# Moving the first batch's feed-forward casts to ScalarE and widening VectorE's third addition of attention weights to the second batch

## The chip, the cores and the metric

The kernel runs on one core of a Trainium2 chip. The metric is the device time of one execution in microseconds (us), the median of several runs. Five engines of the core appear in the profile: TensorE (PE for matmuls, PEld for its weight loads), VectorE (DVE), ScalarE (ACT), GpSimd (POOL) and SyncE (SP, which here only issues transfers). Each works through its own instructions in order, and they wait for one another by semaphores.

## The reference

Two layers follow each other. The first is attention in which a query sees only the keys of its own hash bucket; the second is a feed-forward layer whose hidden values are the largest of three projections.

```python
# q, k, v: (4 batches, 8 heads, 768 positions, 64); proj: (64, 6)
q_bits = (q @ proj > 0);  k_bits = (k @ proj > 0)          # 6 bits give a bucket
mask   = q_bucket[:, :, :, None] == k_bucket[:, :, None, :]
scores = where(mask, q @ k.T / 8, -1e9)
attn   = exp(scores - max);  attn /= attn.sum + 1e-9
x      = (attn @ v) as (3072 tokens, 512)
h      = maximum(maximum(x @ w1, x @ w2), x @ w3)           # w1, w2, w3: (512, 768)
out    = h @ w_out                                          # (768, 512), float32
```

## The kernel before

**Chunks and units.** The queries of a batch are cut into chunks. The first batch (b = 0) has three chunks of 256 queries, c = 0, 1, 2; the other batches have two chunks of 384 each, c = 3 to 8. For each chunk and head, the weights of all 768 keys are made in parts of 768 columns, called units: two units per head in the first batch and three in the others, 48 units per batch and 192 in all. `scores(u)` (line 282) issues three matmuls (256 wide) or two (384 wide) of line 298 into a PSUM tile `sc`, of which there are two, and one exponential on ScalarE (line 306) that writes an fp16 tile `AT`. So the scores of a unit must wait until the exponential of two units before has been read out.

**Sums and values.** When the four heads of a half chunk are done, `burst(c, i)` (line 341) makes their sums of weights with matmuls against a tile of ones (line 358) and the weighted values (line 380). In the first batch the sum takes every one of the six key blocks of a head: 24 matmuls, 32 output rows for each of the four heads. From chunk 3 on, VectorE adds the three units of a head first: `add` (line 322) is called two units after unit 1 and unit 2 of a head and adds whole tiles of 768 columns (line 329). That leaves two blocks of 384 columns per head, so two passes of four matmuls. For chunks from `THIRD_ADD` on, which is 5 here, `add` also adds the two halves to each other (line 332) behind the second addition, and `sum_blocks` (line 334) hands over one block per head: one pass of four matmuls. After the sums VectorE makes reciprocals (lines 365 to 369) and scales the values into `xT` (line 387).

**Feed-forward.** `ffn_groups(c)` (line 402) makes a list of items. An item of the first layer is four matmuls of line 413 for one of six blocks of hidden rows (fb) and one of the three weights (wi) into one of four rotating PSUM banks `ms`. The first weight's result (wi = 0) is cast to fp16 into a tile `ht`; the second and third are taken into it by VectorE's maximum (line 422). The cast is done by ScalarE if the chunk is 384 wide (line 418) and by VectorE if it is 256 wide (line 420). For chunk 0 the items are ordered weight by weight, so that its six casts come from six consecutive items; for the others the three weights of one block follow each other. Items of the second layer are three matmuls of 512 columns (line 457), two items to a row block, with a copy by ScalarE (line 461).

**Order.** The order is written out by hand in the loop over units at the end (line 613). In each turn u it issues `scores(u + 1)`, then whatever is due at u (loads, transposes of later batches by VectorE on line 202, additions), then as many feed-forward items as a credit allows (1 a turn in the first batch, 1.15 afterwards), and last the sums and values that are due. A feed-forward list is appended two turns after the chunk's last values. So the feed-forward of chunk 0 runs in the last units of the first batch, and that of chunks 1 and 2 in the units of the second batch, whose chunks are 3 and 4.

Of the kernel before, what the change touches and what calls it, by code (L numbers as in the profile page):

```python
# [17 lines left out]
def kernel(  # L18
# [12 lines left out]
    nc = tc.nc  # L31
# [4 lines left out]
    HALF = S // 2  # L36
# [15 lines left out]
    EPS = 2.0 ** -60  # L52
    NAT = 24
    SPREAD = {2: (61, 9), 3: (100, 12)}
    THIRD_ADD = 5
    LAG = (1, 4)
    ATW = 776

# [31 lines left out]
    def bank():  # L90
        i = free_banks.pop(0)
        return i, bank_tiles[i]

    def give(i):
        if i is not None:
            free_banks.append(i)
# [182 lines left out]
    def block_of(b, m):  # L279
        return 2 * (m % MH) + m // MH if b == 0 else m  # L280
# [29 lines left out]
    def weights_of(c, h, m):  # L310
        w = chunks[c][2]
        nb = 2 * HALF // w
        return blocks(at_tiles[at_of[unit_at[c, h, m // nb]]], w)[:, m % nb, :]

    def xt_of(c):
        if c not in xts:
            xts[c] = x_pool.tile([P, NJC, HALF], FP16, tag="xT", name="xT")
        return xts[c]
# [3 lines left out]
    def add(c, h, n):  # L322
# [6 lines left out]
        nc.vector.tensor_tensor(out=sum_of[c, h][:], in0=t[0], in1=t[n], op=AluOp.add)  # L329
        if n == 2 and c >= THIRD_ADD:  # L330
            t = sum_of[c, h]
            nc.vector.tensor_tensor(out=t[:, 0, :], in0=t[:, 0, :], in1=t[:, 1, :], op=AluOp.add)  # L332

    def sum_blocks(c, h):
        w = chunks[c][2]
        if (c, h) in sum_of:
            t = sum_of[c, h]
            return [t[:, j, 0:w] for j in range(1 if c >= THIRD_ADD else 2)]
        return [weights_of(c, h, m)[:, 0:w] for m in range(NM)]
# [62 lines left out]
    def ffn_groups(c):  # L402
        b, q0, w = chunks[c]
        xt = xt_of(c)
        hts, gs, l2 = {}, [], {}
        jobs = [(fb, wi) for fb in range(NFB) for wi in range(3)]
        if c == 0:
            jobs = [(fb, wi) for wi in range(3) for fb in range(NFB)]
        for fb, wi in jobs:
            def go(fb=fb, wi=wi):  # L410
                k_, ps = bank()
                for jc in range(NJC):
                    nc.tensor.matmul(ps[:, 0:w], w_sb[wi][:, jc, fb * P : (fb + 1) * P], xt[:, jc, 0:w],  # L413
                                     start=(jc == 0), stop=(jc == NJC - 1))
                if wi == 0:
                    hts[fb] = h_pool.tile([P, HALF], FP16, tag="ht", name="ht")
                    if w == HALF:
                        nc.scalar.copy(hts[fb][:, 0:w], ps[:, 0:w])  # L418
                    else:
                        nc.vector.tensor_copy(hts[fb][:, 0:w], ps[:, 0:w])  # L420
                else:
                    nc.vector.tensor_tensor(out=hts[fb][:, 0:w], in0=hts[fb][:, 0:w], in1=ps[:, 0:w], op=AluOp.max)  # L422
                give(k_)
            gs.append(go)
        rows = out[b * S : (b + 1) * S, :].rearrange("(p c) m -> c p m", c=NM)

        def out_rows(tb):
            if c < NCH - 1:
                return o_pool.tile([P, DM], FP32, tag="osb", name="osb")
            if "end" not in nat:  # L430
                nat["end"] = nat_pool.tile([P, 4 * NM * D], FP32, tag="nat", name="nat")
            return nat["end"][:, tb * DM : (tb + 1) * DM]

        def last(tb, cs, use_act):
            k_, ps = bank()
            n = cs.stop - cs.start
            for fb in range(NFB):
                nc.tensor.matmul(ps[:, 0:n], hts[fb][:, tb * P : (tb + 1) * P], wout_sb[:, fb, cs],  # L438
                                 start=(fb == 0), stop=(fb == NFB - 1))
            osb = out_rows(tb)  # L440
            if use_act:
                nc.scalar.copy(osb[:, cs], ps[:, 0:n])
            else:
                nc.vector.tensor_copy(osb[:, cs], ps[:, 0:n])
            give(k_)
            (nc.scalar if use_act else nc.sync).dma_start(rows[block_of(b, q0 // P + tb)][:, cs], osb[:, cs])

        def item(tb, part):
            def go2(part, tb=tb):
                if c == NCH - 1 and tb == w // P - 1:  # L450
                    last(tb, slice(part * DM // 2, (part + 1) * DM // 2), part == 0)
                    return
                if part == 0:
                    l2[tb] = bank()
                k_, ps = l2[tb]
                for fb in range(part * MH, (part + 1) * MH):
                    nc.tensor.matmul(ps[:, 0:DM], hts[fb][:, tb * P : (tb + 1) * P], wout_sb[:, fb, :],  # L457
                                     start=(fb == 0), stop=(fb == NFB - 1))
                if part == 1:
                    osb = out_rows(tb)  # L460
                    nc.scalar.copy(osb[:, 0:DM], ps[:, 0:DM])  # L461
                    give(k_)
                    nc.sync.dma_start(rows[block_of(b, q0 // P + tb)], osb[:, 0:DM])
            gs.append(lambda: go2(part))

        ntb = w // P
        steps = [(0, 0)]
        for tb in range(1, ntb):
            steps += [(tb, 0), (tb - 1, 1)]
        steps.append((ntb - 1, 1))  # L470
        if c == NCH - 1:
            steps = steps[:-3] + [steps[-2], steps[-3], steps[-1]]
        for tb, part in steps:
            item(tb, part)
        return gs
# [194 lines left out]
```

## Time and profile before

| What | Value |
|---|---|
| Runs before | 264.42, 264.56, 264.79 us; median 264.56 |
| Profiled execution | 264.41 us |
| Span of its instructions | 262.4 us (2.0 us lie around it) |
| Granted TensorE clock | 1.00 |
| Busy | PE 256.5, DVE 207.8, ACT 177.9, POOL 69.8 us |

The profile shows one execution. "Busy" is the time in which at least one instruction of an engine is under way. A timeline row gives start, length, engine, line, operation, output<-input and count; in square brackets stands the idle time of the engine before it and who ended it. Instructions of one engine overlap at their ends, so the distance from one start to the next, called pace below, is shorter than the length that a row gives. A matmul's length is modelled; the starts are what shows how fast TensorE goes.

### The profile page before, as it was taken

To read this page: it belongs to the slowest core of one execution; us is meant where nothing else is said; L and a number is where in the kernel's file an instruction comes from. 1 tells how busy PE (TensorE), PEld (TensorE's weight loads), DVE (VectorE), ACT (ScalarE), POOL (GpSimd) and SP (SyncE) were. 2 spreads that over 40 slices of the span, in tenths; PEclk is the share of its full clock that TensorE was granted. 3 is DMA by queue.
4 is the path that set the end of the run, shared out by engine and by line. 5 is a ranking of instruction groups with operands and counts; after the bars stand their busy time and mean duration, and the time that the engine had idled before them with its cause. 6 is when DMAs were issued, how large, how long until landed. Compare 5 with 4: busy or idle time off the path is not lost.

```text
span 262.4 us, 6477 instructions
## 1 busy us (share of the span) xinstructions
PE 256.5 (98%) x2503; PEld 154.4 (59%) x2503; DVE 207.8 (79%) x492; ACT 177.9 (68%) x258; POOL 69.8 (27%) x132
## 2 busy tenths in 40 slices
PE   8999999999999999999999999999999999999995
PEld 4655658865765666555555554655555555555552
DVE  2897767966799999969999996899849795888350
ACT  3797886667968675956869588584886859581322
POOL 3878752355043526330141612011000000000000
PEclk9999999999999999999999999999999999999999
DMA  6998999979732964970073653802030003000303
GB/s 210 326 224 170 170 235 226 217 132 204 187 91 75 202 139 61 273 186 17 0 198 104 116 127 49 210 0 58 20 122 1 0 2 121 2 0 2 120 0 120
DMA packets 20717, 30.95 MB, mean 118 GB/s; under 512 B 2608, under 2 KB 15248, under 8 KB 20688
## 3 DMA queue, kind: packets, MB, share of 16 engines
q0 software_dynamic: 8128, 13.37, 27.3%
q1 hardware_dynamic: 12128, 16.66, 22.0%
q10 hardware_dynamic: 432, 0.52, 0.6%
q8 instruction: 19, 0.31, 0.5%
q14 instruction: 10, 0.08, 0.1%
HBM read 25.17 MB, written 6.29 MB: 120 GB/s over the span
## 4 chain that ended last, share of the span: by engine, by line
PE 89%; DVE 5%; ACT 3%; issue 2%; DVEq 0%; ACTq 0%
PE ms L413 34%; PE sc L298 22%; PE ms L457 11%; PE ms L380 10%; PE ms L221 3%; ACT AT L306 3%; PE ms L358 3%; PE ms L171 1%; PE ms L123 1%; PE ms L504 1%; DVE ht L422 1%; DVE ad L329 1%; DVE xT L387 1%; PE ms L150 1%; PE ms L438 1%
## 5 line engine op out<-in xcount | busy, mean ns | idle before, releaser
L306 ACT ACTIVATE AT<-sc 128x768 f16<-128x768 f32 x192 | 152.4, 816 | 57.2 <-PE sc L298 53.9
L413 PE MATMUL ms<-xT,w_sb 128*128 128x384 f16 (+1 forms) x648 | 115.0, 307 | 0.3 <-DVE xT L387 0.2
L298 PE MATMUL sc<-S 72*128 72x384 bf16 (+1 forms) x432 | 93.8, 308 | 1.2 <-ACT AT L306 0.9
L413 PEld LDWEIGHTS <-w_sb 128*128 128x128 f16 x648 | 62.7, 97 | 35.9 <-issue 0.4
L422 DVE TENSOR_TENSOR ht<-ht,ms 128x384 f16<-128x384 f16 (+1 forms) x108 | 54.2, 503 | 20.7 <-PE ms L413 10.5
L298 PEld LDWEIGHTS <-S 72*128 72x128 bf16 (+1 forms) x432 | 39.4, 98 | 31.8 <-issue 11.8
L207 POOL TENSOR_SCALAR T<-T 128x768 bf16<-128x768 f32 x24 | 22.8, 951 | 90.2 <-issue 48.4
L457 PE MATMUL ms<-wout_sb,ht 128*128 128x512 f16 x138 | 35.5, 378 | 0.0
L380 PE MATMUL ms<-AT,vo 128*32 128x385 f16 (+3 forms) x840 | 34.2, 308 | 0.0
L380 PEld LDWEIGHTS <-vo 128*32 128x32 f16 x864 | 22.9, 96 | 9.2 <-issue 1.7
L329 DVE TENSOR_TENSOR ad<-ad,AT 128x768 f16<-128x768 f16 x48 | 26.6, 553 | 2.1 <-ACT AT L306 1.3
L202 DVE STREAM_TRANSPOSE T<-nat 128x384 f32<-128x384 f32 x48 | 26.8, 564 | 0.0
L329 DVE TENSOR_TENSOR ad<-AT,AT 128x768 f16<-128x768 f16 x48 | 26.2, 546 | 0.2 <-ACT AT L306 0.2
L418 ACT CAST ht<-ms 128x384 f16<-128x384 f32 x36 | 17.3, 480 | 8.1 <-PE ms L413 8.1
L457 PEld LDWEIGHTS <-ht 128*128 128x128 f16 x138 | 13.3, 97 | 13.0 <-issue 0.3
L387 DVE SCALAR_TENSOR_TENSOR xT<-ms,sv,rb 128x384 f16<-128x384 f32 (+1 forms) x35 | 19.2, 565 | 1.3
L461 ACT COPY osb<-ms 128x512 f32<-128x512 f32 x21 | 12.2, 586 | 7.5 <-PE ms L457 5.8
L332 DVE TENSOR_TENSOR ad<-ad 128x384 f16<-128x384 f16 x32 | 15.5, 484 | 1.1
L137 POOL TENSOR_SCALAR S<-T 64x384 bf16<-64x384 f32 (+1 forms) x23 | 14.1, 616 | 4.9 <-DVE T L132 3.3
L196 POOL DMA_DIRECT2D nat<-in_q_dram x20 | 11.1, 560 | 0.1
L365 DVE STREAM_TRANSPOSE ys<-ms 128x384 f32<-128x384 f32 (+1 forms) x17 | 9.0, 531 | 2.3 <-PE ms L358 2.0
L176 DVE TENSOR_SCALAR S<-ms 6x384 bf16<-6x384 f32 x16 | 8.9, 554 | 2.0 <-PE ms L171 1.2
(52 smaller groups left out, 122.6 us busy)
## 6 DMA issues: line engine op xcount, KB each, us to landing
out_dram<-osb SPq DMA_DIRECT2D x21, 256.0 KB
S<-T SPq DMA_DIRECT2D x48, 96.0 KB
nat<-in_q_dram POOLq DMA_DIRECT2D x20, 192.0 KB, 6.3
vo<-in_v_dram POOLq DMA_DIRECT2D x8, 384.0 KB, 5.8
nat<-in_k_dram POOLq DMA_DIRECT2D x16, 192.0 KB, 5.7
w_sb<-in_moe_w_dram POOLq DMA_DIRECT2D x3, 768.0 KB, 12.8
nat<-in_k_dram SPq DMA_DIRECT2D x10, 192.0 KB
nat<-in_k_dram SPq DMA_DIRECT2D x3, 384.0 KB
```

The lines of the kernel that those rows point to most:

```text
L202: nc.vector.transpose(t32[name][:, u, half * HALF : (half + 1) * HALF], i_)
L207: nc.gpsimd.tensor_scalar(out=t16[name][:, u, :], in0=t32[name][:, u, :], scalar1=RS, scalar2=1.0, op0=AluOp.mult, op1=AluOp.mult)
L298: nc.tensor.matmul(views[j], s_of[kn][0 : D + bits, kx, m * P : (m + 1) * P], s_of[qn][0 : D + bits, qx, q0 : q0 + w], start=True, stop=True)
L306: nc.scalar.activation(t[:, :, 0:w], whole, ActFn.Exp, bias=-SCALE * 0.25 * bits, scale=SCALE)
L329: nc.vector.tensor_tensor(out=sum_of[c, h][:], in0=t[0], in1=t[n], op=AluOp.add)
L332: nc.vector.tensor_tensor(out=t[:, 0, :], in0=t[:, 0, :], in1=t[:, 1, :], op=AluOp.add)
L380: nc.tensor.matmul(av[Q * x : Q * (x + 1), 0:n], v_at[2 * b + i][:, x, cb * D + side : (cb + 1) * D : 2], weights_of(c, 4 * i + x, m)[:, 0 ...
L387: nc.vector.scalar_tensor_tensor(out=xt_of(c)[:, 2 * i + side, 0:w], in0=av[:, 0:w], scalar=sv_of[b, i, side][:], in1=rb[0][:, 0:w], op0=A ...
L413: nc.tensor.matmul(ps[:, 0:w], w_sb[wi][:, jc, fb * P : (fb + 1) * P], xt[:, jc, 0:w], start=(jc == 0), stop=(jc == NJC - 1))
L418: nc.scalar.copy(hts[fb][:, 0:w], ps[:, 0:w])
L422: nc.vector.tensor_tensor(out=hts[fb][:, 0:w], in0=hts[fb][:, 0:w], in1=ps[:, 0:w], op=AluOp.max)
L457: nc.tensor.matmul(ps[:, 0:DM], hts[fb][:, tb * P : (tb + 1) * P], wout_sb[:, fb, :], start=(fb == 0), stop=(fb == NFB - 1))
```

## The change

Two edits are made. All casts of a first weight's result go to ScalarE, also those of the three 256-wide chunks. And `THIRD_ADD` goes from 5 to 3, so that chunks 3 and 4 also get the addition of line 332 and hand over one block per head.

```diff
-    THIRD_ADD = 5
+    THIRD_ADD = 3
...
                 if wi == 0:
                     hts[fb] = h_pool.tile([P, HALF], FP16, tag="ht", name="ht")
-                    if w == HALF:
-                        nc.scalar.copy(hts[fb][:, 0:w], ps[:, 0:w])
-                    else:
-                        nc.vector.tensor_copy(hts[fb][:, 0:w], ps[:, 0:w])
+                    nc.scalar.copy(hts[fb][:, 0:w], ps[:, 0:w])
                 else:
```

The code that reads `THIRD_ADD` is unchanged:

```python
        if n == 2 and c >= THIRD_ADD:                       # in add, line 330
            t = sum_of[c, h]
            nc.vector.tensor_tensor(out=t[:, 0, :], in0=t[:, 0, :], in1=t[:, 1, :], op=AluOp.add)
...
            return [t[:, j, 0:w] for j in range(1 if c >= THIRD_ADD else 2)]   # in sum_blocks, line 338
```

In the instruction lists of the two programs, ScalarE has 18 casts of 128x256 more and VectorE 18 fewer; VectorE has 16 additions of 128x384 more (eight heads of chunk 3 and eight of chunk 4); TensorE has 16 sum matmuls with their 16 weight loads fewer. Nothing else changes its place on any engine, and GpSimd's and SyncE's lists are the same.

## The prediction

> **What bounds the kernel now.** I read the shares of the engines first, then the windows around the change.
>
> ```profile
> span 262.4 us, 6477 instructions
> PE 256.5 (98%) x2503; PEld 154.4 (59%) x2503; DVE 207.8 (79%) x492; ACT 177.9 (68%) x258; POOL 69.8 (27%) x132
> ```
>
> TensorE is the bound: starts in the timeline are 0.11 us apart for 256 columns, 0.16 for 384 and 0.22 for 512, and after 42 us I find only one place (below) where that rhythm breaks by 0.3 us. Work taken from TensorE is saved whole; work moved elsewhere is free until TensorE has to wait. The second row of interest is where the other engines have room, in three windows: the casts of chunk 0, of chunk 1, of chunk 2.
>
> ```profile
> 42.00:47.00 5.00, 4.82 (x45) 4.10 (x44) 3.92 (x12) 5.00 (x7) 1.62 (x5) 1.00 1.17 233
> 66.00:81.00 15.00, 14.86 (x155) 10.65 (x154) 13.59 (x35) 11.75 (x17) 3.51 (x5) 1.00 0.44 116
> 86.00:106.00 20.00, 20.00 (x233) 13.05 (x232) 19.30 (x49) 12.81 (x17) 8.49 (x13) 1.00 0.70 143
> ```
>
> The columns are length, PE, PEld, DVE, ACT, POOL, clock. In the first, ScalarE is busy 5.00 of 5.00 us: just the engine that gets six casts there. In the other two VectorE is close to full (13.59 of 15, 19.30 of 20), and it gets the additions.
>
> **Sums on TensorE: a gain.** In each of the four half chunks of batch 1, two passes of four matmuls become one. The eight matmuls of 72.80 are followed by the values at 73.14, so a pass is 0.17 us, weight loads included. 4 x 0.17 = **-0.67**.
>
> **Chunk 0's casts on ScalarE: a loss.** The timeline there:
>
> ```profile
> 41.91 6.09 ACT L306 ACTIVATE AT<-sc 128x768 f16<-128x768 f32 x8 [3.03 <-PE sc L298]
> ```
> ```profile
> 45.46 0.60 PE L413 MATMUL ms<-xT,w_sb 128*128 128x256 f16 x4
> 45.90 0.49 PE L298 MATMUL sc<-S 70*128 70x256 bf16 x3
> 46.23 0.60 PE L413 MATMUL ms<-xT,w_sb 128*128 128x256 f16 x4
> 46.67 0.49 PE L298 MATMUL sc<-S 70*128 70x256 bf16 x3
> ```
>
> One unit takes TensorE 0.77 us (45.90 to 46.67: 0.33 scores, 0.44 item), and ScalarE starts one exponential per 0.77. Its own limit is 0.71, the distance from an exponential to the next instruction:
>
> ```profile
> 107.75 0.58 ACT L461 COPY osb<-ms 128x512 f32<-128x512 f32 x1
> 108.22 0.83 ACT L306 ACTIVATE AT<-sc 128x768 f16<-128x768 f32 x1
> ...
> 112.31 0.47 ACT L418 CAST ht<-ms 128x384 f16<-128x384 f32 x1
> 112.67 0.83 ACT L306 ACTIVATE AT<-sc 128x768 f16<-128x768 f32 x1
> ```
>
> A 512-wide copy holds ScalarE 0.47 us, a 384-wide cast 0.36; 0.11 less again for 256 wide gives 0.26. The row of a 256-wide copy fits: 0.37 long, against 0.47 to 0.48 for 384 here.
>
> ```profile
> L418 ACT CAST ht<-ms 128x384 f16<-128x384 f32 x36 | 17.3, 480 | 8.1 <-PE ms L413 8.1
> L442 ACT COPY nat<-ms 128x256 f32<-128x256 f32 x1 | 0.4, 372 | 0.1
> ```
>
> With a cast per unit ScalarE needs 0.71 + 0.26 = 0.97 where TensorE gives it 0.77. Step by step: second exponential 42.62 (0.71 after 41.91), first cast 43.33, and from there 0.97 per pair, so the sixth exponential starts at 42.62 + 4 x 0.97 = 46.48. It is 0.81 long, ends at 47.29, and frees the tile for the eighth scores. From the end of an exponential to the scores it frees I find 0.10 to 0.15 where ScalarE sets the pace (17.9 to 18.04, 18.60 to 18.69). The eighth scores so start at 47.41, not 46.67: **+0.75**. The sums and values that follow need no ScalarE and give nothing back; TensorE just does all later work later. Bounds: 0.20 per cast gives +0.5; 0.37, no overlap at all, gives +1.2.
>
> The Trainium skill, "ScalarE: Activation LUTs", section "What ACT_TABLE_LOAD costs", has 186 ns plus 0.833 per element for an instruction with immediate scale and bias, and 93 ns of overlap. By that a 256-wide cast would hold the engine 0.31 us, an estimate, and this term would be +0.95. For 384 it gives 0.51; the trace has 0.48 and a pace of 0.36, so I keep the trace.
>
> **Chunk 1 and 2's casts on ScalarE.** Here one unit in three has a cast. 3 x 0.71 + 0.26 = 2.39 against 3 x 0.77 = 2.30 on TensorE: the first cast after a burst costs about 0.1 (0.26 less the 0.1 of play before scores wait and 0.06 regained per unit), each further one under 0.1, and every turn with two items (credit 1.15) gives 0.44 back. I count +0.3 up to 81 us, +0.1 from 86 to 106, both only if nothing else makes TensorE wait at the same place.
>
> **VectorE in batch 1.** What a third addition costs is shown from chunk 5 on:
>
> ```profile
> 120.45 0.52 DVE L329 TENSOR_TENSOR ad<-ad,AT 128x768 f16<-128x768 f16 x1
> 121.00 0.36 DVE L332 TENSOR_TENSOR ad<-ad 128x384 f16<-128x384 f16 x1
> 121.27 0.55 DVE L422 TENSOR_TENSOR ht<-ht,ms 128x384 f16<-128x384 f16 x1
> ```
>
> It must wait for the addition before it: 0.82 from addition to next instruction, against 0.44 without it (79.99 to 80.42 below). So +0.38 each. A cast frees 0.33 (79.17 to 79.50), or 0.52 where the maximum that reads it stands right behind. Two places decide. The first is the one broken rhythm:
>
> ```profile
> 79.99 0.52 DVE L329 TENSOR_TENSOR ad<-ad,AT 128x768 f16<-128x768 f16 x1
> ...
> 80.26 0.49 PE L298 MATMUL sc<-S 72*128 72x384 bf16 x2
> 80.42 0.94 DVE L422 TENSOR_TENSOR ht<-ht,ms 128x256 f16<-128x256 f16 x2
> ...
> 80.89 0.49 PE L413 MATMUL ms<-xT,w_sb 128*128 128x256 f16 x3
> ```
>
> The item of 80.89 should start at 80.59; it waits for its bank, which the first maximum of 80.42 reads until 80.83. Since its last pause (before 69.41) VectorE would lose three casts (0.52 + 0.33 + 0.33 = 1.18) and gain the third additions of heads 3, 4 and 5 (1.14). The maximum stays where it is, so TensorE's 0.3 of ScalarE waits up to here falls into the 0.30 that it waits now: **0.0** net for chunk 1.
>
> The second is the sum of chunk 4's first half:
>
> ```profile
> 99.39 0.52 DVE L329 TENSOR_TENSOR ad<-ad,AT 128x768 f16<-128x768 f16 x1
> ...
> 100.20 0.51 PE L358 MATMUL ms<-ad,ones 128*32 128x384 f16 x8
> ```
>
> The addition of 99.39 is head 3's second and is done 0.29 before its reader. By then VectorE has lost eight casts since 69.41 (0.52 + 7 x 0.33 = 2.83) and gained eight third additions (3.04): +0.21. Then comes head 3's own third addition, which starts 0.55 later and lasts 0.36: 99.39 + 0.21 + 0.91 = 100.51, and 0.06 for the handover (80.83 to 80.89) make 100.57, not 100.20: **+0.37**, into which ScalarE's 0.1 falls. Queued behind this wait on TensorE are values and everything after. After 100 us the ledger falls back by two more casts, and the last four third additions (1.5 us) meet pauses from 112.9 on. At the three other sums the last addition is done 0.75 us or more before its reader, which covers 0.38.
>
> **At no cost.** No DMA is issued, moved or passed; GpSimd's and SyncE's lists are the same. A bank now released by ScalarE is claimed again four items later, about 3 us, and the cast comes at most 1 us late. VectorE's relief in 42 to 47 us buys nothing, as TensorE doesn't wait for it there.
>
> **Sum.** -0.67 + 0.75 + 0.0 + 0.37 = +0.45. On the profiled execution's own 264.41 (span 262.4 and 2.0 around it) that is **264.9**; the median of the runs shown is 0.15 above that execution. About 0.2%, 0.53 us, is what a measurement can tell from no change.
>
> **Rivals.**
> - *ScalarE's casts are hidden and VectorE is freed (faster).* If VectorE, freed of 0.33 per cast, catches up in TensorE's new pauses, both waits above vanish; and if a cast holds ScalarE 0.18, chunk 0 costs 0.75 - 4 x 0.08 = 0.4: -0.67 - 0.30 + 0.4 = -0.57, 263.8. With 0.26 per cast it would still be -0.22, so the waits on VectorE decide the sign. For it: VectorE, not ScalarE, causes the one wait now seen. Against: it gets as much as it gives, and ScalarE has 5.00 of 5.00. Chance 0.17.
> - *VectorE tips over (slower).* 19.30 of 20 us are busy; if an addition costs 0.5 (two at 84.78 and 107.73 last 1.0, not 0.52, while GpSimd narrows tiles), the ledger is 1.0 worse at 100.20, and the sum there waits 1.2 instead of 0.37: 265.7. It decides from about +0.3 at 99.39 on. Against: TensorE comes later too. Chance 0.28.
> - *The change doesn't do what it says.* The instruction lists show all 18 casts and 16 additions in place and 16 matmuls fewer. Chance 0.02.
>
> The Trainium skill, "ScalarE: Activation LUTs", section "Rules for kernel authors", gives elementwise work to VectorE as the faster engine, which speaks against the move. The rows say otherwise for reads of PSUM: 0.41 us on VectorE, 0.37 on ScalarE for 256 columns. The loss I forecast comes from ScalarE's lack of room, not from its speed.
>
> **How the numbers follow.** The forecast has 0.53 and spans 264.4 to 265.3 (chunk 0 from +0.5 to +1.0, the sum's wait from 0.1 to 0.5); 0.21 of its chance lies over 0.2%, 0.32 within. Of the faster rival 0.12 lies beyond 0.2% and 0.05 within, the slower one wholly beyond, the last within. So faster 0.12, within 0.2% 0.39, slower 0.49. The range, 263.8 to 265.8, reaches to both rivals.
>
> **What would show it.** Scores near 46 us 0.97 apart instead of 0.77, and ScalarE with no idle time; the sums' line with 16 matmuls fewer and 0.17 us between sums and values; a wait of sums for the line 332 near 101 us; chunk 1 with no more waiting than now. Wrong would be: scores still 0.77 apart, or VectorE with pauses between 86 and 106 us.

## The result and the profile after

The changed kernel takes 267.3 us, median of four runs (266.93 to 267.64), beside 264.53 for the kernel before (the three runs shown above and a fourth of 264.50): a ratio of 1.010 with a 95% interval of 1.0083 to 1.0118, or +2.8 us. The forecast was +0.45 (264.9) with a range to 265.8.

The head of the profile of the changed kernel (profiled execution 267.34 us):

```profile
span 265.5 us, 6460 instructions
PE 257.9 (97%) x2487; PEld 154.7 (58%) x2487; DVE 208.7 (79%) x490; ACT 182.0 (69%) x276; POOL 69.8 (26%) x132
```

TensorE has 16 matmuls fewer and yet 1.4 us more of busy time: the end of a matmul is modelled, so part of a wait can stand in a row as work. Where the time went is told by starts. I compared the start of every scores matmul (line 298) in the two profiles; "shift" is how much later it is than before.

| Stretch (time in the profile before) | Change of the shift, us | What stands there |
|---|---|---|
| up to 10 | +0.34 | first loads; differs from execution to execution (-0.13 to +0.63 in the runs below) |
| 44 to 47 | +0.73 | chunk 0's six casts on ScalarE |
| 67 to 70 | +0.34 | chunk 1's first casts on ScalarE |
| 80 to 82 | +0.62 | TensorE waits for VectorE (bank) |
| 92 to 95 | +0.07 +0.45 +0.48 | a cast on ScalarE; twice a bank from VectorE |
| sum at 100.2 | +0.46 | TensorE waits for a third addition |
| the three other sums | -0.17 -0.16 -0.16 | one pass fewer |
| rest | +0.02 | |
| whole span | +3.02 | |

The shorter sums give what was forecast, and chunk 0 costs what was forecast. What is new lies between 80 and 103 us. Busy time there (same columns as in the prediction; the windows are put where the casts of chunks 0, 1 and 2 now run):

```profile
42.00:48.00 6.00, 5.66 (x47) 4.33 (x46) 2.83 (x7) 5.75 (x12) 1.93 (x8) 1.00 1.17 238
66.00:82.00 16.00, 15.92 (x155) 11.10 (x154) 12.91 (x32) 13.83 (x24) 3.54 (x5) 1.00 0.47 122
86.00:109.00 23.00, 22.08 (x236) 14.02 (x234) 22.21 (x52) 15.94 (x26) 10.03 (x14) 1.00 0.63 130
```

In the last window VectorE is busy 22.21 of 23 us (97%), as full as before (19.30 of 20), but about the same work (236 matmuls, 233 before) now fills 23 us instead of 20. TensorE's waits in the changed kernel, by who ended them:

```profile
PE ms L413 <- DVE ht L419: 1.4, 3, 0.8
...
PE ms L358 <- DVE ad L332: 0.3, 1, 0.3
```

Both name VectorE. Its maxima (line 419 here, 422 before) read the PSUM banks that TensorE needs again, and the third addition (line 332) makes the block that a sum reads.

In the chunk 0 stretch the terms of the forecast can be read off, first in ScalarE's rows, then in TensorE's:

```profile
43.65 0.38 ACT L417 CAST ht<-ms 128x256 f16<-128x256 f32 x1
43.90 0.84 ACT L306 ACTIVATE AT<-sc 128x768 f16<-128x768 f32 x1
44.60 0.41 ACT L417 CAST ht<-ms 128x256 f16<-128x256 f32 x1
44.85 0.87 ACT L306 ACTIVATE AT<-sc 128x768 f16<-128x768 f32 x1
```
```profile
45.77 0.49 PE L298 MATMUL sc<-S 70*128 70x256 bf16 x3
46.10 0.60 PE L413 MATMUL ms<-xT,w_sb 128*128 128x256 f16 x4
46.75 0.49 PE L298 MATMUL sc<-S 70*128 70x256 bf16 x3
```

A cast holds ScalarE 0.25 (43.65 to 43.90; 0.26 was estimated), an exponential 0.70, a pair 0.95, and scores come 0.98 apart, 0.97 forecast. No row shows an idle TensorE: the item of four matmuls before each block of scores is drawn 0.60 long, although the next start came after 0.44 in the kernel before (45.46 to 45.90).

The rows that decide are VectorE's at 81 us:

```profile
80.95 0.52 DVE L329 TENSOR_TENSOR ad<-ad,AT 128x768 f16<-128x768 f16 x1
...
81.11 1.04 POOL L207 TENSOR_SCALAR T<-T 128x768 bf16<-128x768 f32 x1 [3.60 <-DVE T L202]
...
81.50 0.86 DVE L332 TENSOR_TENSOR ad<-ad 128x384 f16<-128x384 f16 x1
...
82.29 0.41 DVE L419 TENSOR_TENSOR ht<-ht,ms 128x256 f16<-128x256 f16 x1
...
82.75 0.60 PE L413 MATMUL ms<-xT,w_sb 128*128 128x256 f16 x4 [0.77 <-DVE ht L419]
```

The third addition takes 0.86 us here, not 0.36. It starts at 81.50 while GpSimd narrows a tile, that is, casts transposed queries or keys from fp32 to bf16 (line 207, 81.11 to 82.15). It ends at 82.36, 0.2 after GpSimd has ended. From the start of the addition on line 329 to the maximum it is 1.34 us (80.95 to 82.29) where it was 0.43. The maximum frees a bank that much later, and TensorE stands idle for 0.77. The same pair of rows is at 93.30 and, in front of a sum, at 102.61:

```profile
102.06 0.52 DVE L329 TENSOR_TENSOR ad<-ad,AT 128x768 f16<-128x768 f16 x1
102.22 1.05 POOL L207 TENSOR_SCALAR T<-T 128x768 bf16<-128x768 f32 x1 [3.65 <-DVE T L202]
...
102.61 0.87 DVE L332 TENSOR_TENSOR ad<-ad 128x384 f16<-128x384 f16 x1
...
103.53 0.32 PE L358 MATMUL ms<-ad,ones 128*32 128x384 f16 x1 [0.30 <-DVE ad L332]
```

### The profile page after: what moved, and what is told of

Its sections match the earlier page's. It is cut to its first block, busy times and chain, and to the rows that moved or that the text cites. A ratio compares the mean times of both kernels' runs of the same rounds, so it can differ in the third digit from the quotient of the medians.

```text
span 265.5 us, 6460 instructions
## 1 busy us (share of the span) xinstructions
PE 257.9 (97%) x2487; PEld 154.7 (58%) x2487; DVE 208.7 (79%) x490; ACT 182.0 (69%) x276; POOL 69.8 (26%) x132
## 4 chain that ended last, share of the span: by engine, by line
PE 82%; DVE 9%; ACT 5%; issue 3%; DVEq 0%; ACTq 0%
PE ms L413 31%; PE sc L298 20%; PE ms L380 10%; PE ms L454 10%; ACT AT L306 4%; PE ms L221 3%; PE ms L358 3%; DVE ad L329 3%; DVE ht L419 2%; DVE T L202 2%; PE ms L123 1%; PE ms L171 1%; PE ms L501 1%; DVE xT L387 1%; DVE ad L332 1%
## 5 line engine op out<-in xcount | busy, mean ns | idle before, releaser
L417 ACT CAST ht<-ms 128x384 f16<-128x384 f32 (+1 forms) x54 | 24.5, 454 | 8.2 <-PE ms L413 8.1
L380 PEld LDWEIGHTS <-vo 128*32 128x32 f16 x864 | 23.6, 96 | 9.1 <-issue 2.4
L332 DVE TENSOR_TENSOR ad<-ad 128x384 f16<-128x384 f16 x48 | 23.3, 484 | 1.6
```

The lines of the kernel that those rows point to most:

```text
L380: nc.tensor.matmul(av[Q * x : Q * (x + 1), 0:n], v_at[2 * b + i][:, x, cb * D + side : (cb + 1) * D : 2], weights_of(c, 4 * i + x, m)[:, 0 ...
```

## The experiments

The theory is called V in the first expectations and L in the later ones: sixteen third additions bring VectorE over its limit in batch 1, above all because those that meet a narrowing wait for its end. There are two rivals. By theory S, late casts on ScalarE hold up the maxima behind them. By theory W, the additions are too much by themselves. All differences are between medians, against runs of the kernel before on the same chip; the ratios are not quotients of these medians and can differ from them in the fourth digit. Shifts of starts are counted from 10 us on.

**Third additions alone.** `THIRD_ADD` 3, the casts as before.

```diff
-    THIRD_ADD = 5
+    THIRD_ADD = 3
```

> Third additions from chunk 3 on, all 256-wide casts left on VectorE. Theory V (VectorE falls behind in batch 1, since third additions that start while GpSimd narrows a tile take 0.86 us instead of 0.36): VectorE keeps twelve casts of 0.33 us (4.0 us) on top, so TensorE waits more than in the changed kernel: +3 to +6 us against before (268 to 271). Theory S (ScalarE's casts come late, hold up VectorE's maxima behind them and so the banks): without these casts the waits of 82 to 104 us go: -0.7 to +0.5 us (264.0 to 265.0).

Measured 270.19 beside 264.70: +5.5, ratio 1.0208 (1.0188 to 1.0229). Without a cast of the 256-wide chunks on ScalarE there is more waiting, not less: theory S falls. TensorE's waits, by who ended them:

```profile
PE ms L413 <- DVE ht L422: 3.1, 5, 1.2
...
PE ms L358 <- DVE ad L332: 0.9, 1, 0.9
...
PE ms L457 <- DVE ht L420: 0.3, 1, 0.3
```

**Casts alone.** The changed kernel with `THIRD_ADD` 5.

> All 256-wide casts on ScalarE, third addition from chunk 5 on as before. Theory V: chunk 0 costs 0.72, VectorE is freed of casts and the one wait of 0.30 near 80 us goes, ScalarE costs 0.1 to 0.3 in chunks 1 and 2: +0.4 to +0.8 us (265.0 to 265.3). Theory S: the waits of 82 to 104 us stay: +2.3 to +3.0 us (266.9 to 267.5).

Measured 265.70 beside 264.70: +1.0, ratio 1.0046 (1.0028 to 1.0064), a little above theory V's span. By starts: +0.73 in chunk 0, +0.35 at 67 to 70 us, -0.30 at 81 us. So without third additions in batch 1 ScalarE's waits do fall into the one wait of before, as forecast. A shift of +0.27 at 134 us is the same meeting once more, at the sum of chunk 5's first half:

```profile
132.21 0.86 DVE L332 TENSOR_TENSOR ad<-ad 128x384 f16<-128x384 f16 x1
...
132.83 0.62 PE L358 MATMUL ms<-ad,ones 128*32 128x384 f16 x4
```

The fourth head's addition met a narrowing and ended at 133.07, after the sum had begun; the fourth of the four matmuls starts at 133.12, 0.28 behind the third. In the kernel before the same addition was done 0.09 before its sum.

The two halves are not additive: 5.5 + 1.0 is more than 2.8. Once the additions are there, the casts that VectorE no longer has to do are worth 2.7 us.

**Chunk 0's casts alone.**

```diff
-                    if w == HALF:
+                    if w == HALF or c == 0:
                         nc.scalar.copy(hts[fb][:, 0:w], ps[:, 0:w])
```

> Of the whole change only chunk 0's six casts go to ScalarE. Both theories: scores near 46 us come 0.97 us apart instead of 0.77 and everything behind is 0.7 to 0.75 us later: +0.7 us (265.2). If TensorE makes the time good later, 264.5 to 264.9.

Measured 265.41 beside 264.70: +0.71, ratio 1.0028 (1.0017 to 1.0039). In its trace the shift grows by 0.73 between 44 and 47 us and nothing of it comes back.

**GpSimd's narrowing in two halves.**

```diff
-        nc.gpsimd.tensor_scalar(out=t16[name][:, u, :], in0=t32[name][:, u, :], scalar1=RS, scalar2=1.0, ...)
+        for j in range(2):
+            cs = slice(j * HALF, (j + 1) * HALF)
+            nc.gpsimd.tensor_scalar(out=t16[name][:, u, cs], in0=t32[name][:, u, cs], scalar1=RS, scalar2=1.0, ...)
```

> The whole change, with each of GpSimd's narrowings of 768 columns (line 207) cut into two of 384. Theory V, with the wait lasting to the end of the GpSimd instruction: slow third additions and additions shrink from 0.86 and 1.0 us to 0.65 and 0.8 or less, and TensorE's waits of 82 to 104 us (2.3 us in the changed kernel) to 1.0 to 1.8: +1.5 to +2.3 us against before (266.0 to 266.8). Theory S: no difference from the changed kernel, +2.8 us (267.3).

Measured 267.22 beside 264.70: +2.5, ratio 1.0099 (1.008 to 1.0117). The time missed what theory V expected, the durations did not (line 209 is the narrowing here, 334 the third addition):

```profile
81.59 0.73 POOL L209 TENSOR_SCALAR T<-T 128x384 bf16<-128x384 f32 x1 [0.98 <-DVE T L202]
81.98 0.55 DVE L334 TENSOR_TENSOR ad<-ad 128x384 f16<-128x384 f16 x1
```

The addition again ends 0.2 after GpSimd, at 82.53, and takes 0.55 instead of 0.86. But there are now twice as many narrowings, and they stand apart (72.71 and 75.00, 80.11 and 81.59): from 66 to 108 us nine of VectorE's additions last 0.13 to 0.22 longer than alone, 1.7 us in all, where in the changed kernel four last 0.44 to 0.51 longer, 1.95 in all. TensorE's waits hardly change with that: by starts +0.70 at 81 us and +0.98 at 92 to 95 us, beside 0.62 and 0.93.

**GpSimd without the narrowing.** A fill with zeros takes its place, so these kernels leave out the transposed queries and keys; the order of instructions on VectorE and TensorE stays.

```diff
-        nc.gpsimd.tensor_scalar(out=t16[name][:, u, :], in0=t32[name][:, u, :], ...)
+        nc.gpsimd.memset(t16[name][:, u, :], 0.0)
```

> The whole change, but GpSimd fills each narrowed tile with zeros (memset, which reads nothing) instead of narrowing what VectorE transposed: the queries and keys of half of batch 1's heads' successors, batches 1 to 3 as far as they go this way, are left out of the computation, the instruction order on VectorE and TensorE is the same. Theory L (lock: VectorE's additions with two inputs in SBUF wait for GpSimd's read of SBUF to end, and these 0.5 us waits push VectorE over): no addition above 0.6 us, TensorE's waits of 82 to 104 us fall from 2.3 to 1.2 or less: +1.2 to +1.8 us against before (265.9 to 266.5). Theory W (the sixteen additions by themselves are too much for VectorE, the lock adds nothing): +2.5 to +2.8 us (267.2 to 267.5).

> The kernel before, with GpSimd filling the narrowed tiles with zeros instead of narrowing (the transposed queries and keys from batch 1's second half on are left out of the computation): the control for the same edit on the changed kernel. Theory L: in the kernel before only two additions of batch 1 meet a narrowing, behind the one wait near 80 us; so 0 to -0.4 us (264.1 to 264.5). If the edit gained by another way, such as earlier transfers, it would gain here the 1.9 us that it gained on the changed kernel (262.6).

With the zero fill the changed kernel takes 265.36 beside 264.48: +0.9, ratio 1.0033 (1.0022 to 1.0044), less than even theory L expected. The kernel before does not gain by the same edit: 264.70 beside 264.64, ratio 1.0006 (0.9995 to 1.0018). All 48 third additions now take the short time (line 331 here), and one wait of TensorE is left in batch 1:

```profile
L331 DVE TENSOR_TENSOR ad<-ad 128x384 f16<-128x384 f16 x48 | 17.2, 358 | 1.6
```
```profile
81.18 0.36 DVE L331 TENSOR_TENSOR ad<-ad 128x384 f16<-128x384 f16 x1
81.28 1.43 POOL L207 MEMSET T<- 128x768 bf16 x2
81.46 0.94 DVE L418 TENSOR_TENSOR ht<-ht,ms 128x256 f16<-128x256 f16 x2
81.93 0.27 PE L412 MATMUL ms<-xT,w_sb 128*128 128x256 f16 x1 [0.33 <-DVE ht L418]
```

So 1.9 of the 2.8 us hang on additions that meet the narrowing. Theory W falls for the changed kernel.

**Third additions alone, without the narrowing.**

> Third additions from chunk 3 on, casts of the 256-wide chunks left on VectorE, and GpSimd filling the narrowed tiles with zeros (the transposed queries and keys from batch 1's second half on are left out of the computation). It tells how the 5.5 us that the additions cost without the moved casts divide into GpSimd's lock and VectorE's plain load. Theory L: the lock is worth about 2 to 3 us here too, the rest is load: +2.5 to +3.5 us against before (267.1 to 268.1). If the load alone does it, +5 us (269.6); if the lock alone, +0.5 us or less.

Measured 268.10 beside 264.76: +3.3, ratio 1.0124 (1.0107 to 1.0141). Of the 5.5 us that the additions cost with the casts on VectorE, 2.2 are the meeting with GpSimd and 3.3 plain load. So theory W has a large part in this kernel. With the casts moved as well, the load alone nearly fits: of the +0.9, starts show about 1.15 for the casts on ScalarE (0.73, 0.35, 0.07) and 0.36 for VectorE's lateness (0.19, 0.05, 0.12), less 0.65 at the sums.

**Third additions one turn later.**

```diff
-        if n == 2 and c >= THIRD_ADD:
-            t = sum_of[c, h]
-            nc.vector.tensor_tensor(out=t[:, 0, :], in0=t[:, 0, :], in1=t[:, 1, :], op=AluOp.add)
...
                 when(min(u + 2, NU - 1), add, c, h, n)
+                if n == 2 and c >= THIRD_ADD:
+                    when(min(u + 3, NU - 1), third, c, h)
```

> The whole change, with each third addition issued one turn later, so that in most cases a maximum stands between it and the addition that it reads. Theory L: no wait for the addition before (0.1 us each) and a shorter one for GpSimd, and the maxima that free banks come first: +1.0 to +1.8 us against before (265.7 to 266.5). Theory W: a few tenths less than the changed kernel, +2.3 to +2.7 us.

Measured 265.84 beside 264.48: +1.4, ratio 1.0046 (1.0034 to 1.0059). In batch 1 two of the long additions come down to 0.65, the maxima go first, and TensorE no longer waits for a bank there. One wait stays, at the sum, behind an addition that still meets the narrowing (lines 333 and 359 here):

```profile
101.01 0.86 DVE L333 TENSOR_TENSOR ad<-ad 128x384 f16<-128x384 f16 x1
...
101.93 0.32 PE L359 MATMUL ms<-ad,ones 128*32 128x384 f16 x1 [0.44 <-DVE ad L333]
```

**The same with chunk 0's casts back on VectorE** (`if c > 0` ahead of ScalarE's copy).

> As the kernel with the later third additions, and chunk 0's six casts back on VectorE. Both theories: 0.7 us less than that kernel, as chunk 0's casts alone cost 0.7; so +0.3 to +1.1 us against before by theory L (265.0 to 265.8), +1.6 to +2.0 by theory W.

Measured 265.05 beside 264.48: +0.6, ratio 1.0017 (1.0006 to 1.0028). That is 0.8 less than with them on ScalarE, as the run of chunk 0 alone (0.71) had let expect.

**In search of a faster version.** From there, no third addition for chunk 4's first four heads, and then also chunk 1's first two casts on VectorE:

```diff
+    def has_third(c, h):
+        return c >= THIRD_ADD and not (c == 4 and h < 4)
...
-                    if c > 0:
+                    if c > 1 or (c == 1 and fb >= 2):
```

> Chunk 0's casts on VectorE, those of chunks 1 and 2 on ScalarE, third additions one turn later, but none for chunk 4's first four heads, whose sum waited 0.45 us near 102 us. Theory L: that wait goes (-0.6 with what follows it), one pass of 0.17 comes back: 0.2 to 0.5 us less than with them, -0.2 to +0.2 us against before (264.3 to 264.7). If VectorE is too full anyway, the wait comes elsewhere: +0.5 us (265.0).

> As the kernel before this one in the list, and chunk 1's first two casts, at 66 and 69 us, on VectorE, which has idle time just there, while ScalarE's casts made the scores wait 0.34 us there. Theory L: 0.3 us less than skip_half, -0.6 to -0.1 us against before (263.9 to 264.4), the first version below both kernels. If VectorE is pushed over by them, 0 to +0.5 us more than skip_half.

Measured 264.41 and 264.54 beside 264.64: ratios 0.9994 (0.9981 to 1.0008) and 0.9997 (0.9982 to 1.0013). Neither can be told from the kernel before, and the 0.3 us that the second was to gain on the first does not show. In the second one's trace no wait of TensorE for VectorE is named in batch 1 (two starts near 81 us still come 0.14 and 0.13 late), and from 10 us to the end it is 0.32 us shorter than the kernel before; the medians do not confirm that. In the first one's profile TensorE waits 0.7 us near 141 us for an exponential. It stands behind a copy of ScalarE that waits 1.13 us for an output tile to be written out (139.24); why that transfer was late stays open.

## Why the prediction was wrong, step by step

- **Sums, -0.67: right.** 0.16 to 0.17 at each of the three sums that wait for nothing, 16 matmuls fewer.
- **Chunk 0's casts, +0.75: right.** 0.73 in the changed kernel, +0.71 by themselves, 0.25 per cast: the trace's pace held. The estimate from the Trainium skill, "ScalarE: Activation LUTs", section "What ACT_TABLE_LOAD costs" (0.31 per cast, +0.95) was too high here.
- **ScalarE in chunks 1 and 2, 0.3 and 0.1: right in size** (0.34 and 0.07). That the first part falls into VectorE's wait at 80 us and leaves "0.0" for chunk 1 held only with the casts alone (-0.30 there); with the third additions that wait grew by 0.62 instead of vanishing. Chunk 1's two parts came to +0.96.
- **The third addition, "+0.38 each": the step that failed.** I priced it from one timeline row of 0.36 us (121.00). The group row of the kernel before said otherwise, and so did single rows of it:

```profile
L332 DVE TENSOR_TENSOR ad<-ad 128x384 f16<-128x384 f16 x32 | 15.5, 484 | 1.1
```
```profile
124.05 0.98 POOL L207 TENSOR_SCALAR T<-T 128x768 bf16<-128x768 f32 x1 [10.49 <-issue]
...
124.38 0.86 DVE L332 TENSOR_TENSOR ad<-ad 128x384 f16<-128x384 f16 x1
```

A mean of 484 ns does not come from rows of 0.36 alone: 24 of the 32 take 0.36 and 8 take 0.86, and each of the eight starts while line 207 runs. In the changed kernel the three that meet a narrowing before 103 us (81.50, 93.30, 102.61) cost 0.9 each (80.95 to 82.29 is 1.34, less 0.43) and not 0.38: 1.5 us more of VectorE's time than the forecast had. Without the narrowing the change costs 1.9 us less.

- **"Two places decide": wrong with it.** A VectorE that is late by 0.5 more at 81 and 93 us makes TensorE wait for banks at 94 and 96 us too (+0.45 and +0.48), where I saw no wait. The largest wait was at 81 us, the place I took as settled. This step is off even without the narrowing: there VectorE's wait at 81 us grows by 0.19 where -0.30 was forecast, the banks at 94 and 96 us cost 0.05, and the sum waits 0.12, not 0.37. Two errors partly cancel, and +0.9 comes out instead of +0.45. Of the signs that the prediction named, only this one did not come: chunk 1 with no more waiting than now.
- **The sum at 100.2, +0.37: too small.** It waits 0.62 (0.46 net of the pass that it saves), behind the same kind of long addition.
- **The slower rival had the mechanism** (additions that last longer while GpSimd narrows tiles), but with a chance of 0.28, and with 1.2 us at one sum instead of four waits. Its own terms, 0.37 + 1.0, would have made 1.4 and 265.9. It could have been settled from the trace of before.
- **Small slips that change nothing:** 42.62 + 4 x 0.97 is 46.50, not 46.48, and 3 x 0.77 is 2.31. The forecast's own span comes to 264.3 to 265.2 from its bounds. TensorE's rhythm also breaks at 42.72 in the kernel before, where it stands 0.18 for `xT`; the change does not touch that.

The Trainium skill, "SBUF — State Buffer", section "SBUF: two separate sides", says that a VectorE operation with two inputs in SBUF and a GpSimd operation that reads SBUF exclude one another, whoever starts first holding the ports for its whole instruction. The rows agree: every third addition that starts within a narrowing ends 0.2 us after it (81.50, 102.61), halving the narrowing shortens the wait (0.86 to 0.55), and with a fill that reads nothing the wait is gone (0.36). They agree for the other order too: a narrowing takes 0.83 us in the first batch, where no addition is under way, and 1.05 when it starts with 0.36 us of an addition left, as at 102.22. By that page the long rows were to be expected, and it should have been one of the rivals.

## What to carry to other kernels

When a row's mean does not match the instance one looks at, there are others that last longer: find what the long ones stand beside before pricing a copy of them. For an engine that is 97% busy a price per operation does not add up to the cost: here half a microsecond more became a wait wherever its late results held a bank, so look at every buffer, not only at the two tightest readers. Moving load off such an engine and adding load to it are not additive: here the moved casts cost 1.0 us alone and gained 2.7 beside the additions.

## What the runs showed of the hardware

- VectorE's fp16 additions with both inputs in SBUF wait for a GpSimd tensor_scalar under way: 0.86 instead of 0.36 us for 384 columns, 1.0 instead of 0.52 to 0.56 for 768. They end 0.2 us (384 columns) and 0.4 us (768) after GpSimd's row. All 12 third additions of 0.86 us in the changed kernel start within a narrowing, none of the 36 of 0.36 us does. Maxima with one input in PSUM that start within one (0.38 to 0.42 us) and transposes (0.53 to 0.57) are not slowed: those that start outside one take as long.
- The wait goes the other way as well. In the changed kernel GpSimd's narrowing of 768 columns takes 0.82 to 0.83 us when no such addition is under way (8 of 24, all in the first batch), 0.98 when it starts with 0.28 to 0.29 us of one left, and 1.04 to 1.05 with 0.35 to 0.36 left.
- GpSimd's zero fill does not slow these additions: third additions that start within one take 0.36.
- ScalarE's rows grow from 0.38 to 0.51 (casts) and from 0.84 to 0.98 (exponentials) along the chunk 0 stretch of the changed kernel, while the pace stays 0.25 and 0.70: the length of a row is not what an operation costs.
